# A causal convolution and a GELU layer on one core: five buffers for convolved blocks, all first taps on ScalarE, and half of one sum by transfer

## Chip, core and metric

The kernel runs on one core of a Trainium2 chip. The metric is device microseconds of one execution. The engines are named as in the profile: PE is the TensorE's matmuls (PEld its weight loads), DVE is VectorE, ACT is ScalarE, POOL is GpSimd, SP is SyncE, which here only issues transfers.

## What is computed

The input x has 8 sequences of 4096 tokens with 192 channels. Each of 8 heads (24 channels) has seven weights, which are normalized by a softmax; every channel is convolved with them over the last seven tokens. The result goes through a layer of 2048 hidden values with an exact GELU.

```python
w = np.exp(weight - np.max(weight, axis=-1, keepdims=True))
w = w / (np.sum(w, axis=-1, keepdims=True) + 1e-09)           # (8 heads, 7 taps)
x_pad = np.concatenate([np.zeros((B, 6, D)), x], axis=1)
idx = np.arange(S)[:, None] + np.arange(7)[None, :]
x_unf = x_pad[:, idx, :].reshape(B, S, 7, H, 24)
y = np.einsum('hk,bskhg->bshg', w, x_unf).reshape(B * S, 192)
h = y @ w_in                                                  # (32768, 2048)
g = 0.5 * h * (1.0 + erf(h / sqrt(2)))
out = g @ w_out                                               # (32768, 192), float32
```

## The kernel before, in words

**Blocks.** The 32768 tokens are cut into two halves that are worked on side by side, and each half into 35 blocks: blocks 0 to 5 with 256 tokens, blocks 6 to 34 with 512. Channels lie on partitions, the two halves together fill 128 partitions, and 192 channels make three planes of 64.

**Stages of a block n.** (1) SP loads x into one of three buffers `xin` (`load`). (2) DVE transposes it into `xT` (`trans`, written `tN` in the order), and POOL copies the six tokens before the block to its head (`halo`). (3) Seven taps make the convolution: the first tap multiplies into `acc`, six more multiply and add (`tap`, L345), and the last writes bf16 into `xc`. A first tap is made by DVE (L340), in two pieces, or by ACT (`first_tap`, L1123), one piece for each plane, written `f0`, `f1`, `f2`; which is set by `AT1` and `CALLS`. For blocks 0 and 1 PE makes the convolution. (4) The first product, `mm1` (L1258), multiplies `xc` with `win` in 16 slices into two PSUM buffers `hp` that alternate; after each slice ACT applies the GELU (L1165) and writes `gT`. (5) The second product of block n-1 is put piece by piece between the slices of block n. (6) Its result is transposed by DVE out of PSUM into `osb` (the `ev` steps), and SP stores it.

**Two kinds of second product.** From block 6 to 33, ten blocks make it directly (`mm2_t`, L1343, 48 rounds of four matmuls). The 18 blocks of the list `ST` make it with seven products instead of eight, in the manner of Strassen (`mm2_s`, L1392, 44 rounds). For those, sums of the GELU results are needed beforehand. They are cut into pieces of the eight column groups:

- `S1.0`, `S1.1`, `S1.2`: sum of two quarters of `gT`, by DVE (L699).
- `S3.0`, `S3.1`: one quarter of `gT` is added to another by an accumulating transfer that POOL issues (L671); `S3.2` is made by DVE (L702).
- `Dn.0`, `Dn.1`: a quarter plus `S1`. `Dn.1` is made by DVE (L705). `Dn.0` comes by transfer where the block before is a direct one (nine blocks): POOL copies the quarter (`cp`, L682) and then adds `S1` with an accumulating transfer (L686). In the other nine blocks DVE makes it (L705).
- `S4.0`, `S4.1`: a quarter plus `Dn`, by DVE (L708).

The products are named P1 to P7, D, E and e in `UNIT`; `TILES` gives the order in which each quarter of the PE works them off, in parts of which 5.5 make a block's second product. P6 reads Dn, P3 reads S4, P7 reads S3, P5, E and e read S1, and P4 needs the step k0. Afterwards the results are combined: ACT copies `p15`, `e`, `u`, `p3` out of PSUM (L743), POOL sends `u` across partitions twice (`cu` into `uu` and `cg` into `gsm` or `p5s`, L666), and DVE makes `k0` (L751), `k4` (L764, frees a PSUM bank, waits for `cg`) and `k3` (L758, waits for `cu`).

**What sets the order.** Each engine works its instructions off in the order of the program. For DVE it is written out by hand in `LIST`: row n holds the taps of block n (the bare digits), the transposes `tN`, and the steps of earlier blocks, `name.piece.block`. For ACT, `SLOT` says before which GELU of a block an extra instruction stands (`10:f1.13` before GELU 10). For POOL it is `GLIST`. SP loads some blocks ahead and then stores block n-1, in one loop; a load waits until DVE has transposed the block that had its buffer. A tap 6 waits until the first product of the last block with the same `xc` buffer is done:

```python
dst = ap(xc[n % 2], p0 * TB, [[NP * TB, 128], [TB, pn], [1, w]])
e.wait_ge(S_MM1, SL0[n - 1])
```

A copy `cp` waits, among others, until S4 of the seven-product block before is made, since all share one buffer `Dn`.

Of the kernel before, what the change touches and what calls it, by code (L numbers as in the profile page):

```python
# [11 lines left out]
def bass_lightweight_conv__then__act_gelu_exact_kernel(  # L12
# [91 lines left out]
    SLOT = {
        7: "2:f0.9 3:f1.9 5:f2.9",
        8: "3:f0.10 3:f1.10 6:f2.10 13:f0.11",
        9: "5:f1.11 6:p15.8 10:f2.11 13:f0.12 14:e.8",
        10: "0:f1.12 2:u.8 3:p3.8 4:f2.12 6:f0.13 10:f1.13",
        11: "1:f2.13 6:p15.10 13:e.10",
        12: "0:p3.10 2:u.10 6:p15.11 8:f2.14 11:f0.15 13:e.11 14:f1.15",  # L110
        13: "1:p3.11 2:u.11 4:f2.15 11:f0.16",
        14: "1:f1.16 4:f2.16 6:p15.13 9:f2.17 14:e.13",
        15: "0:p3.13 2:u.13 6:p15.14 13:e.14",
        16: "0:u.14 2:p3.14 4:f0.18 6:f1.18 8:f2.18 10:f0.19 13:f1.19",
        17: "7:p15.16 10:f2.19 12:f2.20 14:e.16",
        18: "0:p3.16 2:u.16 6:p15.17 13:e.17",
        19: "0:u.17 2:f0.21 4:p3.17 6:f1.21 8:f2.21",
        20: "5:f0.22 6:p15.19 10:f1.22 10:f2.22 13:e.19 14:f2.23",
        21: "0:p3.19 2:u.19 6:p15.20 13:e.20 15:f0.24",
        22: "2:u.20 4:p3.20 5:f1.24 8:f2.24 11:f0.25",  # L120
        23: "5:f1.25 6:p15.22 10:f2.25 13:e.22 14:f0.26",
        24: "0:u.22 2:p3.22 4:f1.26 4:f2.26 12:f0.27",
        25: "1:f1.27 4:f2.27 6:p15.24 14:e.24",
        26: "0:p3.24 2:u.24 6:p15.25 11:f2.28 13:f0.29 14:e.25",
        27: "0:p3.25 2:f1.29 4:u.25 6:f2.29",
        28: "0:f0.30 2:f1.30 6:p15.27 10:f2.30 13:f0.31 14:e.27",
        29: "0:f1.31 2:f2.31 3:u.27 4:p3.27 8:f0.32 10:f1.32 13:f2.32",
        30: "6:p15.29 14:e.29",
        31: "0:p3.29 2:u.29 4:f0.33 7:p15.30 8:f1.33 9:f2.33 13:e.30",
        32: "0:p3.30 2:u.30 4:f0.34 7:p15.31 9:f1.34 10:f2.34 15:e.31",  # L130
        33: "0:p3.31 2:u.31 6:p15.32 13:e.32",
# [58 lines left out]
    with es:  # L190
# [17 lines left out]
        xc = [sbt("xc%d" % i, [128, NP * TB], BF16) for i in range(2)]  # L208
# [450 lines left out]
        def st_dma(e, m, name, q):  # L659

            if name in ("cu", "cg"):
# [4 lines left out]
                e.dma_start(dst[UP, :], uu[LO, :]).then_inc(S_AD[name], 16)  # L666
                return
            if name == "S3":
# [842 lines left out]
```

## Time and profile before

| | |
|---|---|
| median of 3 runs | 666.59 us (666.11 to 667.13) |
| the profiled execution | 666.53 us, span of its instructions 664.8 us |
| busy: PE, DVE, ACT, POOL | 658.9, 623.6, 591.1, 105.5 us |
| granted TensorE clock | 1.00 |
| first GELU of blocks 31, 32, 33, 34 | 570.87, 591.87, 611.76, 631.65 us |
| GELU (L1165), mean of one | 1022 ns, 510 counted |
| tap on DVE (L345, 128x1536), mean of one in 84 to 632 us | 1806 ns |
| first tap on ACT (L1123, 128x512), mean of one | 714 ns |

The span runs from the first to the last instruction of the program; the rest of the execution's time lies around it. Busy time of PE is the union of matmuls that overlap in a pipeline, and so says little on how much faster PE could be. A row of the profile gives line, engine, operation, tiles and shapes, then the count, busy time, mean duration, and the idle time in front with what ended it.

### The profile page before, as it was taken

How to read it: one execution, taken by the hardware profiler on the slowest of the kernel's cores; microseconds unless marked ns; L12 is line 12 of the kernel's file. 1: busy time of each engine (PE TensorE's matmuls, PEld its weight loads, DVE VectorE, ACT ScalarE, POOL GpSimd, SP SyncE). 2: the span in 40 equal slices, each digit the busy share in tenths (PEclk: the TensorE clock that was granted, in tenths of full speed). 3: DMA queues.
4: the chain of work that ended last, by engine and by line, in shares of the span. 5: the costliest groups of instructions: out<-in, count | busy, mean ns of one | idle time of the engine just before them, and what ended most of it. 6: DMA issues, size and time to landing. Idle time of an engine off the chain costs nothing.

```text
span 664.8 us, 27970 instructions
## 1 busy us (share of the span) xinstructions
PE 658.9 (99%) x12792; PEld 478.9 (72%) x12792; DVE 623.6 (94%) x564; ACT 591.1 (89%) x691; POOL 105.5 (16%) x175
## 2 busy tenths in 40 slices
PE   9999999999999999999999999999999999999997
PEld 8999655576776677778777666757666757677776
DVE  5989999999999999999999999999999999999962
ACT  8899988898899898989889998989898998999882
POOL 8000540102010110202120102110102030111010
DMA  9746675645914691596189145959245838352454
GB/s 156 162 96 133 109 121 122 136 98 130 216 40 113 156 193 34 138 206 124 38 192 221 34 106 120 195 115 225 45 98 136 184 82 192 66 113 50 92 134 112
DMA packets 146438, 83.66 MB, mean 126 GB/s; under 512 B 129936, under 2 KB 138192, under 8 KB 146320
## 3 DMA queue, kind: packets, MB, share of 16 engines
q1 hardware_dynamic: 129328, 49.42, 33.7%
q0 software_dynamic: 15872, 31.86, 23.7%
q8 instruction: 100, 1.64, 1.0%
q10 hardware_dynamic: 1120, 0.59, 0.3%
q14 instruction: 18, 0.15, 0.1%
HBM read 31.51 MB, written 25.17 MB: 85 GB/s over the span
## 4 chain that ended last, share of the span: by engine, by line
PE 94%; DMA 2%; DVE 2%; POOL 1%; issue 1%; ACT 0%; DVEq 0%; POOLq 0%; ACTq 0%
PE hp L1258 48%; PE ob L1392 25%; PE ob L1343 16%; PE ob L1298 4%; DVE acc L345 1%; PE hp L1448 1%; DMA win<-in_moe_w_in_dram 1%; DMA xin<-in_x_dram 1%; PE ob L1448 1%; DMA uu<-uu 0%; ACT gT L1165 0%; POOL win L839 0%; DVE xT L984 0%; POOL xTb L360 0%; DVE xc L345 0%
## 5 line engine op out<-in xcount | busy, mean ns | idle before, releaser
L1165 ACT ACTIVATE gT<-hp 128x1024 bf16<-128x1024 f32 x510 | 514.6, 1022 | 60.1 <-PE hp L1258 52.7
L1258 PE MATMUL hp<-xc,win 64*64 64x512 bf16 (+2 forms) x6036 | 432.6, 366 | 0.5 <-DVE xc L345 0.4
L1258 PEld LDWEIGHTS hp<-xc,win 64*64 64x64 bf16 (+1 forms) x6036 | 229.1, 105 | 88.6 <-ACT gT L1165 5.9
L345 DVE SCALAR_TENSOR_TENSOR acc<-xT,wcol,acc 128x1536 f32<-128x1536 f32 (+1 forms) x165 | 282.3, 1711 | 7.4 <-ACT acc L1123 4.6
L1392 PE MATMUL ob<-gT,wot 64*64 64x512 bf16 x1152 | 219.6, 376 | 0.0
L1392 PE MATMUL ob<-gT,wst 64*64 64x512 bf16 (+2 forms) x1152 | 203.1, 323 | 0.7 <-DVE p5s L764 0.7
L1343 PE MATMUL ob<-gT,wot 64*64 64x512 bf16 x1920 | 133.5, 376 | 0.0
L1392 PE MATMUL ob<-s_S,wot 64*64 64x128 bf16 (+2 forms) x864 | 132.5, 305 | 0.0
L1392 PEld LDWEIGHTS ob<-gT,wst 64*64 64x64 bf16 x1152 | 98.5, 107 | 16.3 <-DVE p5s L764 1.6
L1392 PEld LDWEIGHTS ob<-gT,wot 64*64 64x64 bf16 x1152 | 89.5, 107 | 10.9 <-DVE osb L776 0.5
L1343 PEld LDWEIGHTS ob<-gT,wot 64*64 64x64 bf16 x1920 | 63.9, 107 | 39.7 <-DVE osb L776 0.3
L1392 PEld LDWEIGHTS ob<-s_S,wot 64*64 64x64 bf16 x864 | 68.6, 107 | 15.9
L1392 PE MATMUL ob<-s_Dn,wst 64*64 64x512 bf16 x288 | 79.5, 376 | 0.0
L1392 PE MATMUL ob<-s_S,wst 64*64 64x512 bf16 x288 | 79.5, 376 | 0.0
L671 POOL DMA_DIRECT2D gT<-gT x36 | 32.1, 902 | 198.3 <-DVE s_S L699 198.3
L984 DVE STREAM_TRANSPOSE xT<-xin 128x1536 f32<-128x1536 f32 (+2 forms) x39 | 59.4, 1532 | 3.5 <-DMA xin<-in_x_dram 2.8
L345 DVE SCALAR_TENSOR_TENSOR xc<-xT,wcol,acc 128x1536 bf16<-128x1536 f32 (+1 forms) x33 | 56.7, 1717 | 0.8
L1123 ACT ACTIVATE acc<-xT,wcol 128x512 f32<-128x512 f32 (+1 forms) x77 | 53.5, 698 | 0.0
L699 DVE TENSOR_TENSOR s_S<-gT 128x1024 bf16<-128x1024 bf16 (+1 forms) x54 | 45.8, 853 | 2.6 <-PE ob L1392 1.2
L708 DVE TENSOR_TENSOR s_S<-gT,s_Dn 128x2048 bf16<-128x2048 bf16 x36 | 43.1, 1218 | 0.4
L1298 PE MATMUL ob<-wout,gT 64*128 64x192 bf16 x768 | 42.0, 243 | 0.0
L892 POOL COPY xT<-xT 128x18 f32<-128x18 f32 x29 | 14.9, 514 | 156.8 <-DVE xc L345 145.1
(92 smaller groups left out, 416.1 us busy)
## 6 DMA issues: line engine op xcount, KB each, us to landing
out_dram<-osb SPq DMA_DIRECT2D x124, 192.0 KB, 3.5
xin<-in_x_dram SPq DMA_DIRECT2D x116, 192.0 KB, 4.2
gT<-gT POOLq DMA_DIRECT2D x18, 512.0 KB, 5.1
s_Dn<-gT POOLq DMA_DIRECT2D x9, 512.0 KB, 2.9
gT<-gT POOLq DMA_DIRECT2D x18, 256.0 KB, 4.1
s_Dn<-s_S POOLq DMA_DIRECT2D x9, 512.0 KB, 5.6
uu<-uu POOLq DMA_DIRECT2D x18, 128.0 KB, 2.6
xin<-in_x_dram SPq DMA_DIRECT2D x18, 96.0 KB, 2.5
```

Source lines behind the costliest of these rows:

```text
L345: return e.scalar_tensor_tensor(dst, src, wk, a, op0=ALU.mult, op1=ALU.add)
L671: e.dma_start(quad(m, 1, 0, k, k1 - k), quad(m, 0, 0, k, k1 - k), accum_op=ALU.add).then_inc(S_AD["S3.%d" % q], 16)
L699: ins = v.tensor_tensor(t("S1"), quad(m, 1, 0, k, n), quad(m, 1, 1, k, n), ALU.add)
L708: ins = v.tensor_tensor(t("S4"), quad(m, 0, 1, k, n), t("Dn"), ALU.add)
L892: g.tensor_copy(dst, src).then_inc(S_HALO)
L984: v.transpose(out, src).then_inc(S_TR)
L1123: a.activation(out=acc[n % 2][:, p * TB : p * TB + w], in_=ap(xT[n % 2], p * XW + HX, [[NP * XW, 128], [1, w]]), func=AF.Copy, scale=wcol[ ...
L1165: a.activation(out=ap(gT[n % 2], (i % 2 * NF + i // 2) * TB if n in ST else i * c * 2 * w, dst), in_=ap(ob, 2 * TB, [[4 * TB, 128], *src[1 ...
L1258: ins = t.matmul(hbuf(u, slice(fo, fo + fw), o, w), ap(win, f1, [[NP * F, 64], [2, fw]]), xc[n % 2][r, p * TB : p * TB + w], start=(p == 0 ...
L1298: ins = t.matmul(bb[sub], gT[m % 2][r, c0 : c0 + 128], wout[r, CH[sub][i] * C : (CH[sub][i] + 1) * C], start=(ph == 0 and k == 0), stop=(p ...
L1343: ins = t.matmul(bank(BK[m][j], slice(64 * h, 64 * h + 64), w), ap(wot, 64 * hf * NF * C + CH[h][i] * C + 64 * j, [[NF * C, 64], [1, 64]]) ...
L1392: ins = t.matmul(bank(BK[m][bk], slice(64 * cg, 64 * cg + 64))[:, c0 : c0 + w], wt_, x, start=(e == mine[0]), stop=(e == mine[-1] or e in ...
```

## The change

- `xc` has five buffers instead of two; tap 6 of block n waits for the first product of block n-5.
- ACT makes all three first tap pieces of every block from 4 on (93 instead of 77). DVE made both pieces for blocks 7 and 8 and one piece for 14, 17, 20, 23 and 28.
- `Dn.0` comes by transfer in all 18 seven-product blocks. Every second one uses a buffer of its own, `dn2`; `u` is also kept in two buffers in turn, `uu` and `u2`, each with its own semaphores.
- `LIST` now begins at row 4 and holds the preparation of the weights (`w`) and the evictions of block 5, which stood in a list of their own; `LIST`, `SLOT` and `GLIST` are written anew. SP's lead is given for each block in `AHEAD`.

`c1` and the transfer of `S1` in the new code are issued by no entry of the lists. The core of the diff, with the rows that the prediction speaks of:

```diff
+    NXC = 5
+    AHEAD = {4: 10, 6: 13, 7: 14, 8: 14, 9: 16, 10: 18, 11: 18, 12: 20, 13: 20, 14: 20, 15: 22, 16: 22, 17: 23, 18: 25, 19: 25, 21: 27, 22: 28, 23: 30, 24: 30, 26: 33, 27: 35, 28: 35, 29: 35}
...
+        4: "w.0.0 t5 1 w.1.0 2 3 4 5 6",
+        5: "t6 1 2 3 4 5 6",
+        6: "1 t7 2 3 w.2.0 w.3.0 4 5 w.4.0 6",
+        7: "1 2 3 4 5 t8 w.5.0 w.6.0 6",
+        8: "t9 evac.0.5 evac.1.5 w.7.0 1 2 3 4 w.8.0 w.9.0 ev.0.6 5 6",
...
-        32: "ev.0.27 Dn.1.29 S4.0.29 S3.2.29 ev.2.28 1 S4.1.29 2 k0.0.29 S1.0.30 3 t33 4 ev.2.29 Dn.0.30 S1.1.30 S1.2.30 5 6",
-        33: "S3.2.30 k3.0.29 k4.0.29 Dn.1.30 S4.0.30 S4.1.30 ev.1.29 ev.0.29 k0.0.30 1 S1.0.31 2 ev.2.30 S1.1.31 3 S1.2.31 t34 S3.2.31 Dn.0.31 4 k4.0.30 Dn.1.31 S4.0.31 S4.1.31 k3.0.30 k0.0.31 5 6",
-        34: "S1.0.32 S1.1.32 1 ev.2.31 ev.0.30 S1.2.32 Dn.0.32 S4.0.32 Dn.1.32 ev.1.30 S3.2.32 k4.0.31 S4.1.32 2 3 k0.0.32 4 5 S1.0.33 k3.0.31 6",
+        32: "ev.1.28 S1.2.29 Dn.1.29 ev.2.28 k3.0.27 ev.1.27 S3.2.29 1 S4.0.29 S4.1.29 2 k0.0.29 3 S1.0.30 4 5 S1.1.30 ev.2.29 t33 S1.2.30 Dn.1.30 S3.2.30 6",
+        33: "k4.0.29 S4.0.30 k3.0.29 ev.0.29 S4.1.30 ev.1.29 k0.0.30 t34 1 S1.0.31 S1.1.31 2 ev.2.30 3 S1.2.31 4 5 S3.2.31 k4.0.30 Dn.1.31 S4.0.31 S4.1.31 k0.0.31 k3.0.30 ev.0.30 ev.1.30 6",
+        34: "S1.0.32 S1.1.32 1 ev.2.31 2 S1.2.32 S3.2.32 3 Dn.1.32 k4.0.31 4 ev.0.31 S4.0.32 S4.1.32 k0.0.32 k3.0.31 ev.1.31 5 S1.0.33 6",
...
+        7: "1:f0.8 2:f1.8 3:f2.8 8:f0.9 9:f1.9 11:f2.9",
+        12: "0:p3.10 2:u.10 4:f0.14 6:p15.11 8:f1.14 9:f2.14 13:e.11 14:f0.15",
+        31: "0:p3.29 2:u.29 4:f0.33 6:p15.30 8:f1.33 10:f2.33 12:f0.34 13:e.30",
...
-        xc = [sbt("xc%d" % i, [128, NP * TB], BF16) for i in range(2)]
+        xc = [sbt("xc%d" % i, [128, NP * TB], BF16) for i in range(NXC)]
+        dn2 = sbt("dn2", [128, NF // 4 * TB], BF16)
+        u2 = sbt("u2", [128, TB], F32)
...
-                dst = ap(xc[n % 2], p0 * TB, [[NP * TB, 128], [TB, pn], [1, w]])
-                e.wait_ge(S_MM1, SL0[n - 1])
+                dst = ap(xc[n % NXC], p0 * TB, [[NP * TB, 128], [TB, pn], [1, w]])
+                if n >= NXC:
+                    e.wait_ge(S_MM1, SL0[n - NXC + 1])
...
-        BYDMA = {'N': 'S3.0 S3.1 Dn.0', 'S': 'S3.0 S3.1'}
+        BYDMA = {'N': 'S3.0 S3.1 Dn.0', 'S': 'S3.0 S3.1 Dn.0'}
...
-                if ST.index(m):
-                    e.wait_ge(*summed(ST[ST.index(m) - 1], "S4", k))
+                j = ST.index(m) - 2 + min(q, 1)
+                if j >= 0:
+                    e.wait_ge(*summed(ST[j], "S4", k))
...
-            "cu.0.25 cp.0.27 cg.0.25 S3.0.27 Dn.0.27 S3.1.27 halo.31 halo.32 cg.0.27 "
-            "cu.0.27 cp.0.29 S3.0.29 S3.1.29 Dn.0.29 halo.33 S3.0.30 S3.1.30 cu.0.29 "
-            "cg.0.29 S3.0.31 S3.1.31 cg.0.30 cu.0.30 halo.34 S3.0.32 S3.1.32 cg.0.31 "
-            "cu.0.31 S3.0.33 S3.1.33 cg.0.32 cu.0.32 cg.0.33 cu.0.33 "
+            "cu.0.27 S3.0.29 cp.0.29 Dn.0.29 S3.1.29 halo.32 halo.33 cp.0.30 S3.0.30 "
+            "Dn.0.30 S3.1.30 cg.0.29 cu.0.29 halo.34 cp.0.31 S3.0.31 S3.1.31 Dn.0.31 "
+            "cg.0.30 cu.0.30 cp.0.32 S3.0.32 S3.1.32 cg.0.31 Dn.0.32 cu.0.31 cp.0.33 "
+            "S3.0.33 S3.1.33 cg.0.32 Dn.0.33 cu.0.32 cg.0.33 cu.0.33 "
...
-                while xs < min(NB, n + 5 + (1 if n >= 8 else 0)):
+                while xs < min(NB, AHEAD.get(n, n + 5)):
```

More of the change, by code (lines that the diff above doesn't have):

```diff
@@ L75, in bass_lightweight_conv__then__act_gelu_exact_kernel @@
     LIST = {
[27 rows of a table removed]
[32 rows of a table added]
     }
     SLOT = {
[L105 to L112, printed above, removed]
-        15: "0:p3.13 2:u.13 6:p15.14 13:e.14",
@@ L114, in bass_lightweight_conv__then__act_gelu_exact_kernel @@
[L114 to L131, printed above, removed]
+        2: "3:f0.4 5:f1.4 6:f2.4",
@@ new lines, in bass_lightweight_conv__then__act_gelu_exact_kernel @@
+        3: "1:f0.5 3:f1.5 4:f2.5 7:f0.6",
+        4: "1:f1.6 3:f2.6",
+        5: "1:f0.7 3:f1.7 6:f2.7",
+        7: "1:f0.8 2:f1.8 3:f2.8 8:f0.9 9:f1.9 11:f2.9",
+        8: "2:f0.10 3:f1.10 7:f2.10",
+        9: "1:f0.11 6:p15.8 9:f1.11 10:f2.11 12:f0.12 13:e.8 15:f1.12",
+        10: "1:p3.8 3:f2.12 3:u.8 6:f0.13 8:f1.13 9:f2.13",
+        11: "7:p15.10 13:e.10",
+        12: "0:p3.10 2:u.10 4:f0.14 6:p15.11 8:f1.14 9:f2.14 13:e.11 14:f0.15",
+        13: "0:p3.11 3:u.11 4:f1.15 5:f2.15 7:f0.16 11:f1.16",
@@ new lines, in bass_lightweight_conv__then__act_gelu_exact_kernel @@
+        14: "0:f2.16 7:p15.13 10:f0.17 10:f1.17 13:e.13 14:f2.17",
+        15: "0:p3.13 2:u.13 6:p15.14 13:e.14",
+        16: "0:f0.18 2:p3.14 3:u.14 5:f1.18 6:f2.18 9:f0.19 11:f1.19",
+        17: "3:f2.19 6:p15.16 10:f0.20 10:f1.20 13:e.16 14:f2.20",
+        18: "0:p3.16 2:u.16 6:p15.17 14:e.17 15:f0.21",
+        19: "0:u.17 2:p3.17 3:f1.21 5:f2.21 8:f0.22 9:f1.22 11:f2.22",
+        20: "6:p15.19 10:f0.23 11:f1.23 13:e.19 14:f2.23",
+        21: "0:p3.19 2:u.19 6:p15.20 13:e.20",
+        22: "1:p3.20 4:u.20 4:f0.24 6:f1.24 9:f2.24 10:f0.25",
@@ new lines, in bass_lightweight_conv__then__act_gelu_exact_kernel @@
+        23: "3:f1.25 6:p15.22 9:f2.25 12:f0.26 13:e.22 15:f1.26",
+        24: "1:f2.26 3:u.22 4:p3.22 7:f0.27 11:f1.27",
+        25: "1:f2.27 6:p15.24 13:e.24 14:f0.28",
+        26: "0:p3.24 2:u.24 6:p15.25 8:f1.28 9:f2.28 13:e.25 14:f0.29",
+        27: "1:p3.25 4:u.25 4:f1.29 6:f2.29 9:f0.30",
+        28: "4:f1.30 7:p15.27 8:f2.30 9:f0.31 14:e.27 15:f1.31",
+        29: "1:u.27 2:f2.31 4:p3.27 8:f0.32 12:f1.32",
+        30: "3:f2.32 6:p15.29 14:e.29",
+        31: "0:p3.29 2:u.29 4:f0.33 6:p15.30 8:f1.33 10:f2.33 12:f0.34 13:e.30",
@@ L132, in bass_lightweight_conv__then__act_gelu_exact_kernel @@
+        32: "0:p3.30 2:u.30 6:p15.31 10:f1.34 10:f2.34 15:e.31",
+        33: "0:p3.31 2:u.31 7:p15.32 13:e.32",
         34: "0:p3.32 2:u.32 7:p15.33 15:e.33 15:u.33",
@@ L135, in bass_lightweight_conv__then__act_gelu_exact_kernel @@
     SLOT = {n: [(int(i), k, int(m)) for i, k, m in (q.replace(":", ".").split(".") for q in s.split())] for n, s in SLOT.items()}
-    AT1 = {4: (3, 5, 6), 5: (3, 5, 6), 6: (2, 3, 5)}
-    for n in range(M0 + 3, NB):
+    AT1 = {}
+    for n in range(4, NB):
         AT1[n] = [(b, i) for b in SLOT for i, k, m in SLOT[b] if k[0] == "f" and m == n]
@@ L263, in bass_lightweight_conv__then__act_gelu_exact_kernel @@
         S_DP = sem("S_DP")
-        S_AD = {k: sem("S_AD" + k) for k in ("S3.0", "S3.1", "S3.2", "Dn.0", "Dn.1", "cp.0", "cp.1", "cu", "cg")}
+        S_AD = {k: sem("S_AD" + k) for k in ("S3.0", "S3.1", "S3.2", "S1.0", "c1.0", "Dn.0", "Dn.1", "cp.0", "cp.1", "Dn.0b", "cp.0b", "cu", "cg", "cub", "cgb")}
         block = es.enter_context(nc.Block())
@@ L306, in conv_out @@
             o = p * TB + c0 + d0
-            dst = xc[n % 2][ro, o : o + dw]
+            dst = xc[n % NXC][ro, o : o + dw]
             cb = 512 * cbank(n, kd) + d0
@@ L562, in bass_lightweight_conv__then__act_gelu_exact_kernel @@
                     key, one = (p, 16) if p in BYDMA[m] else (name, 1)
+                    if p == "Dn.0" and one > 1:
+                        key += "b" * (ST.index(m) % 2)
                     count[key] = count.get(key, 0) + one
@@ L568, in summed @@
             return SUM_AT[m, name, [k < q for q in SUMS[name][1:]].index(True)]
-        SIDE = [((M0 + 2, 4 * g // 2, 0), "evac", M0 - 1, g) for g in range(NG[M0 - 1])]
-        SIDE += [((M0 - 1, 2 * k + 1, 0) if k < NP else (M0 + 1 + (k - NP) // 4, 2 + (k - NP) % 4, 0), "w", 0, k) for k in range(10)]
-        SIDE.sort(key=lambda q: q[0])
+        SIDE = []
         for b in LIST:
@@ L647, in quad, with sums @@
             return ap(gT[m % 2], ((2 * par + h) * (NF // 2) + k) * TB, [[NF * 2 * TB, 128], [1, n * TB]])
+        def sums(m, name, k, n, r=slice(0, 128), c0=0):
+            if name == "Dn" and k < NF // 4 and ST.index(m) % 2:
+                return dn2[r, k * TB + c0 :][:, :n]
+            return sst[name][r, k * TB + c0 :][:, :n]
         def st_read(e, m, name, q):
-            if m - 1 in ST and (name, q) in FORM[m - 1][5]:
+            if m - 1 in ST and (name, q) in FORM[m - 1][5] and (name, q) != ("Dn", 0):
                 EVENTS, _, DONE, _, _, READ = FORM[m - 1]
@@ L664, in st_dma @@
                     e.wait_ge(S_DP, dp(m, "k0"))
-                dst = uu if name == "cu" else gs(m)
-                e.dma_start(dst[UP, :], uu[LO, :]).then_inc(S_AD[name], 16)
+                dst = us(m) if name == "cu" else gs(m)
+                e.dma_start(dst[UP, :], us(m)[LO, :]).then_inc(S_AD[name + "b" * (ST.index(m) % 2)], 16)
                 return
@@ L674, in st_dma @@
                 return
+            if name in ("c1", "S1"):
+                k, k1 = SUMS["S1"][q : q + 2]
+                d = ap(sst["S1"], k * TB, [[NF // 2 * TB, 128], [1, (k1 - k) * TB]])
+                if name == "c1":
+                    e.wait_ge(S_GELU, SL0[m] + 2 * k1)
+                    st_read(e, m, "S1", q)
+                    if ST.index(m):
+                        e.wait_ge(*summed(ST[ST.index(m) - 1], "Dn", k))
+                    e.dma_start(d, quad(m, 1, 0, k, k1 - k)).then_inc(S_AD["c1.%d" % q], 16)
+                else:
+                    e.wait_ge(S_AD["c1.%d" % q], SUM_AT[m, "S1", q][1])
+                    e.dma_start(d, quad(m, 1, 1, k, k1 - k), accum_op=ALU.add).then_inc(S_AD["S1.%d" % q], 16)
+                return
             k, k1 = SUMS["Dn"][q : q + 2]
-            d, s1 = (ap(sst[x], k * TB, [[NF // 2 * TB, 128], [1, (k1 - k) * TB]]) for x in ("Dn", "S1"))
+            odd = "b" * (q == 0 and ST.index(m) % 2)
+            d, s1 = (sums(m, x, k, (k1 - k) * TB) for x in ("Dn", "S1"))
             if name == "cp":
@@ L693, in t @@
             def t(x):
-                return ap(sst[x], k * TB, [[NF // 2 * TB, 128], [1, n * TB]])
+                return sums(m, x, k, n * TB)
             v.wait_ge(S_GELU, SL0[m] + 2 * k1)
@@ L713, in gs, with us @@
             return (gsm, p5s)[ST.index(m) % 2]
+        def us(m):
+            return (uu, u2)[ST.index(m) % 2]
         def tqs(m):
@@ L731, in st_copy @@
                     "p15": (gs(m)[:, :], bank(BK[m]["X"])),
-                    "u": (uu[LO, :], xb(LO)),
+                    "u": (us(m)[LO, :], xb(LO)),
                     "p3": (tqs(m)[LO, :], xb(UP)),
@@ L739, in st_copy @@
                 a.wait_ge(S_EV, EV[ST[i - 2], 1])
-            if name == "u" and i:
-                a.wait_ge(S_DP, dp(ST[i - 1], "k3"))
-                a.wait_ge(S_AD["cg"], 16 * i)
+            if name == "u" and i > 1:
+                a.wait_ge(S_DP, dp(ST[i - 2], "k3"))
+                a.wait_ge(S_AD["cg" + "b" * (i % 2)], 16 * (i // 2))
             a.activation(out=dst, in_=src, func=AF.Copy, scale=-1.0 if name == "p15" else 1.0).then_inc(S_AC)
@@ L752, in st_post @@
             elif name == "k3":
-                v.wait_ge(S_AD["cu"], 16 * ST.index(m) + 16)
+                v.wait_ge(S_AD["cu" + "b" * (ST.index(m) % 2)], 16 * (ST.index(m) // 2) + 16)
                 v.wait_ge(S_AC, ac(m, "p3"))
@@ L758, in st_post @@
                 ins = v.scalar_tensor_tensor(
-                    tqs(m)[:, :], uu[:, :], sgn[:, 0:1], tqs(m)[:, :], op0=ALU.mult, op1=ALU.add
+                    tqs(m)[:, :], us(m)[:, :], sgn[:, 0:1], tqs(m)[:, :], op0=ALU.mult, op1=ALU.add
                 )
@@ L762, in st_post @@
                 v.wait_ge(S_MM2, MMC[m + 1])
-                v.wait_ge(S_AD["cg"], 16 * ST.index(m) + 16)
+                v.wait_ge(S_AD["cg" + "b" * (ST.index(m) % 2)], 16 * (ST.index(m) // 2) + 16)
                 ins = v.tensor_tensor(gs(m)[:, :], bank(BK[m]["Y"]), gs(m)[:, :], ALU.subtract)
@@ L1008, in _ @@
             for n in range(2, NB):
-                if n < M0 + 3:
+                if n < 4:
                     ops = [] if n in K0 else [("t", n, 0)]
@@ L1063, in extra @@
                     st_add(v, n, name, q)
-            side = [q for q in SIDE if q[0][0] < M0 + 3]
+            side = [q for q in SIDE if q[0][0] < 4]
             for b in range(2, NB):
@@ L1112, in _ @@
             first = {}
-            for n, at in AT1.items():
-                if n < M0 + 1:
-                    for j, q in enumerate(at):
-                        first[n - 2, q] = (n, j)
             def first_tap(n, p):
@@ L1260, in mm1 @@
                                 ap(win, f1, [[NP * F, 64], [2, fw]]),
-                                xc[n % 2][r, p * TB : p * TB + w],
+                                xc[n % NXC][r, p * TB : p * TB + w],
                                 start=(p == 0 and (cc == 0 or not head)),
@@ L1382, in mm2_s @@
                     need(*summed(m, src, k))
-                    x = sst[src][r, k * TB + c0 :][:, :w]
+                    x = sums(m, src, k, w, r, c0)
                 g = CG[0][k]
```

6 lines of the change are left out of this document (3 added, 3 removed), and 68 rows, old and new, of tables (GLIST, LIST).

## The prediction

> **What bounds the kernel now.** I read the page's first part, then the chain of waits in order of time for the pace of TensorE (PE), then busy time by stretches of one block, then the timeline where one stretch is longer than its like.
>
> ```profile
> PE 658.9 (99%) x12792; PEld 478.9 (72%) x12792; DVE 623.6 (94%) x564; ACT 591.1 (89%) x691; POOL 105.5 (16%) x175
> ...
> 110.36 0.86 PE ob L1343 x16
> 111.22 0.65 PE hp L1258 x12
> ```
>
> Matmuls overlap, so 99% busy alone proves nothing. The pace does: 16 matmuls of 512 columns in 0.86 us, 12 in 0.65, hence 54 ns each while one lasts 376 ns: four quarters of the array work at once, 0.215 us for each four, at granted clock 1.00. What can be won is therefore only time in which PE stands still. To find it I compare block periods (first GELU of a block to the next one's first GELU). Each of the two stretches below holds 192 first-product matmuls and one seven-product sum:
>
> ```profile
> 570.87:591.87 21.00, 20.28 (x406) 14.38 (x401) 19.46 (x20) 18.98 (x23) 3.76 (x5) 1.00 0.41 90
> 591.87:611.76 19.89, 19.89 (x406) 15.59 (x399) 19.76 (x19) 18.96 (x24) 3.11 (x5) 1.00 0.26 52
> ```
>
> Columns: length, then busy time and count of PE, PEld, DVE, ACT, POOL. The same 406 matmuls take 1.11 us more in block 31. Summing such differences over blocks 7 to 33 (like against like, from the times between the ends of first-product groups) I find 0.93 + 0.25 in block 31, 0.12 in block 12, 0.09 in block 17, and nothing else over 0.08 us. The stall itself:
>
> ```profile
> 573.57 0.56 POOL L666 DMA_DIRECT2D uu<-uu  x1 [1.29 <-ACT uu L743]
> 574.16 0.56 POOL L666 DMA_DIRECT2D p5s<-uu  x1
> ...
> 576.87 0.75 DVE L758 SCALAR_TENSOR_TENSOR wtf<-uu,sgn,wtf 128x512 f32<-128x512 f32 x1 [1.08 <-DMA uu<-uu]
> 577.54 0.68 DVE L764 TENSOR_TENSOR p5s<-ob,p5s 128x512 f32<-128x512 f32 x1
> ...
> 578.28 0.35 PE L1392 MATMUL ob<-gT,wst 64*64 64x128 bf16 x2 [0.72 <-DVE p5s L764]
> ```
>
> POOL issues cu.0.29 before cg.0.29; VectorE (DVE) runs k3.0.29 (L758), which waits 1.08 us for cu, before k4.0.29 (L764), and PE waits 0.72 us for the bank that k4 frees. So PE is the bound, with some 1.4 us of stalls in 550; DVE, 94% busy, has hardly any slack (its last convolved block ends at 630.17, 0.3 us before PE wants it), which is why single delays reach PE.
>
> **The sum** starts at the profiled execution: 666.53 us, its span of 664.8 and 1.7 around it. The median of the three runs is 666.59, so no correction.
>
> **First taps to ScalarE (ACT).** Removed from DVE (L340): seven of 128x1024 and two of 128x512, 7 x 0.71 + 2 x 0.47 = 5.9 us. Added to ACT: 16 of 128x512.
>
> ```profile
> L1123 ACT ACTIVATE acc<-xT,wcol 128x512 f32<-128x512 f32 x68 | 48.3, 714 | 0.0
> L705 DVE TENSOR_TENSOR s_Dn<-gT,s_S 128x2048 bf16<-128x2048 bf16 x25 | 30.2, 1211 | 0.1
> ```
>
> 16 x 0.71 = 11.4 us on ACT. Cover: it sits idle 52.7 us in front of GELUs waiting for PE. The fullest new block (12, as 31) has 16 GELUs, 4 first taps and p3, u, p15, e. Two GELUs take 1.94 us in the timeline, one 1.02, so the pitch is 0.92; with the same 0.1 off the others: 14.7 + 2.4 + 1.6 = 18.7, under the 19.9 of a block. Block 7 gets six taps, 18.4 of 20.7. Three of them stand ahead of successive GELUs; ACT then falls behind by 3 x (0.92 + 0.61 - 1.29) = 0.7 us, and the two hp buffers allow some 0.9 (two turns of 1.29 less a first product of 0.65 and a GELU of 1.02). On the path: 0. Without that cover each further tap would cost PE 0.6.
>
> **Half of Dn by transfer in nine more blocks.** DVE sheds 9 x 1.21 = 10.9 us (L705). POOL gets nine cp (0.55 to issue) and nine Dn (1.03), 14.2 us, of which its 16% load makes nothing. What counts is order. Behind a Dn waiting for its cp to land stand S3, cg and cu; and transfers issued on top of each other are slow:
>
> ```profile
> gT<-gT POOLq DMA_DIRECT2D x18, 512.0 KB, 5.1
> s_Dn<-gT POOLq DMA_DIRECT2D x9, 512.0 KB, 2.9
> s_Dn<-s_S POOLq DMA_DIRECT2D x9, 512.0 KB, 5.6
> ...
> DMA to landing us min/median/max: 4.5/5.6/7.9
> ```
>
> The last line is Dn's (L686): 7 to 8 when issued within 1 us of an S3, 4.5 to 5.3 mostly otherwise. In most blocks P6, the reader of Dn, starts some 12 us into the next block, and 7 us or more are left: 0. The chain that is short is Dn, S4, P3 in the run of seven-product blocks 29 to 33, where the new list puts Dn.0.32 behind cg.0.31. That moment stands in the trace:
>
> ```profile
> 613.58 0.58 ACT L743 ACTIVATE uu<-ob 64x512 f32<-64x512 f32 x1
> 614.52 0.56 POOL L666 DMA_DIRECT2D p5s<-uu  x1 [4.60 <-ACT uu L743]
> 615.12 0.55 POOL L666 DMA_DIRECT2D uu<-uu  x1
> ```
>
> p5s<-uu is cg.0.31; Dn.0.32 takes the place of the next line, 615.1. Landing 4.5 to 5.3 later: 619.6 to 620.4. S4.0.32 (L708, 1.22): 620.8 to 621.6. Need: P3 starts at 2.75 of the 5.5 parts of block 33's PE time, which begins at about 611.1 (first GELU 611.76 less 0.65): 621.0. DVE reaches S4.0.32 at about 620.0 (ev.2.31 at 611.0, then four taps of 1.8 and five small operations). So 0 to 0.6 us of stall here and, by the same order (cg.0.32 ahead of Dn.0.33), 0 to 0.5 in block 34. With Dn at 7.9 it would be 3.2 and some 3. Nothing excludes a gain, but PE has nothing to gain here beyond the stalls counted below. I take 0.2 for both together, since no S3 is issued within 4 us of either Dn.
> [...]
>
> **New order on DVE and POOL at block 31.** The new lists put cg.0.29 ahead of cu.0.29 and k4.0.29 ahead of k3.0.29. cg then issues at 573.57, lands 2.2 (its median) to 3.0 later (as here), 575.8 to 576.6; k4 ends by 576.4 to 577.3; PE ran dry between 577.1 and 577.6. Gain 0.9 to 1.1; I take 1.1. S1.1.30, whose S3 is queued ahead of cg, now has 6.5 us of DVE work between it and k4, more than the 4.5 of that issue and landing. Blocks 12 and 17: 0.1 of 0.2.
>
> **Five xc buffers.** Tap 6 of block n waits for first products of n-5, not n-2. In the trace DVE never waits there (before xc it is idle 0.8 us in 33). The list still does block n beside the sums of n-2, so the lead doesn't grow: 0. **Second buffers** u2, dn2: u and cp wait one seven-product block less; POOL's early waits aren't on the path: 0. **Loads ahead (SP).** A store now stands behind later loads. Worst: store of block 26 behind load 34, which waits for t31; that is 5.4 us of DVE work after ev.1.26, and its buffer is wanted two lists later: 0. **Weights and block 6's evictions earlier.** DVE waits 3.0 us at 45.3 for a first tap of block 5, which now comes earlier; that pays for the three w of list 4 to 6 (0.34 to 0.61 each). xc of block 6 ends near 65.6 instead of 66.2. In list 8, ev.0.6 waits for PE's second pass over block 6, with taps 5 and 6 behind it: xc of block 8 near 101.4, wanted at 104.5: 0.
>
> Sum: 666.53 - 1.1 - 0.1 + 0.2 = 665.5.
>
> **Rivals.**
> (1) DVE is the bound and its 16.8 us come off: 649.7. For: 94% busy, no slack. Against: PE's pace is the same in every block, and block 32 shows DVE busy 19.76 of 19.89 with PE never still. Chance 0.02. [...]
> (2) The stall at block 31 stays or moves, since a transfer from POOL lands late elsewhere (uu<-uu took 7.8 in one place): 666.5. Chance 0.14. Equally if the change doesn't do what it says and leaves DVE's turn as it was.
> (3) Slower: Dn queued against S3. Where Dn.0 stands straight ahead of S3.0 (blocks 11, 24, 27), S3.0 lands in up to 8.0 instead of 5.1, and Dn in 7.9. From a landing of 5.0 on, each us costs one in block 33 and one in block 34; S3.0.24 (issue near 443.9, wanted near 451.0) adds up to 0.9. All at the maximum: 666.53 - 1.2 + 3.2 + 3.0 + 0.9 = 672.4; with half of it 668.9. It decides from a mean landing of 6.3, where it costs 2.5 and the forecast's gain of 1.2 is outweighed by 1.3. Chance 0.20.
>
> **Numbers.** Forecast 0.64, spread 664.8 to 666.0. A measurement here tells about 0.2%, 1.33 us, from no change; so faster means under 665.2. Of the forecast's chance 0.30 lies below that, 0.34 above; rival 1 adds 0.02 to faster, rival 2 0.14 to same, rival 3 0.04 to same and 0.16 to slower. Faster 0.32, same 0.52, slower 0.16. The range runs from the forecast's lower end, 664.8, to 667.9, so leaving out rival 1 and most of rival 3.
>
> **What would show it.** Right: block 31 takes 19.9 us, no PE wait on k4; DVE falls to near 607 us busy with waits of its own, ACT rises to about 602; PE's pace unchanged. Wrong: a PE wait for s_S or s_Dn in blocks 33 and 34, S3 landings over 6 in blocks 11, 24, 27, or ACT late in block 7.

## The result: 0.7% slower, and where PE stands still now

The changed kernel takes 671.38 us (median of 6 runs, 670.32 to 672.82), the kernel before 666.78 beside it: ratio 1.0072, interval 1.0059 to 1.0085. The profiled execution took 671.19 us with a span of 669.5, 4.7 more than before. 665.5 was forecast, with a range to 667.9.

The engines' instruction counts changed as planned: 18 fewer on DVE, 16 more on ACT, 18 more on POOL. The first line of the page:

```profile
PE 660.9 (99%) x12792; PEld 486.7 (73%) x12792; DVE 611.1 (91%) x546; ACT 598.8 (89%) x707; POOL 122.8 (18%) x193
```

DVE is 12.5 us less busy (16.8 were forecast), ACT 7.7 (11.4) and POOL 17.3 (14.2) more, and the kernel is slower all the same. PE's pace is unchanged: block 7 takes 20.72 us in both. From the first GELU of block 7 to that of block 34 the changed kernel takes 551.8 us, 547.1 before; these 4.7 us are the whole loss. Against the shortest like time between the ends of first-product groups, block 12 loses 2.2 us, 32 1.1, 21 0.9, 31 0.8; 20, 25, 30 and 33 lose 0.4 to 0.5 each. Together PE loses some 8 us in blocks 7 to 33, some 3 before (where the prediction listed the larger ones, 1.4). Block 12 from first GELU to first GELU, before and after:

```profile
187.04:206.43 19.39, 19.39 (x394) 13.65 (x390) 19.13 (x18) 18.31 (x23) 1.43 (x5) 1.00 0.16 33
186.64:208.59 21.95, 20.45 (x405) 14.18 (x399) 19.17 (x18) 19.52 (x24) 2.19 (x3) 1.00 0.76 170
```

Before, PE was busy throughout; now it is busy for 20.45 of 21.95 us. The last two numbers say that the DMA engines were 16% busy and moved 33 GB/s in this block, and now are 76% busy and move 170. Block 31, the place of the old stall, in the timeline:

```profile
576.80 0.56 POOL L686 DMA_DIRECT2D p5s<-u  x1 [2.82 <-ACT u L782]
...
580.57 0.69 DVE L803 TENSOR_TENSOR p5s<-ob,p5s 128x512 f32<-128x512 f32 x1 [1.96 <-DMA p5s<-u]
...
581.32 0.35 PE L1428 MATMUL ob<-gT,wst 64*64 64x128 bf16 x2 [0.51 <-DVE p5s L803]
```

cg.0.29 is now issued first, as planned, but it lands at 580.47, 3.7 us after its issue; DVE sits idle for 1.96 us in front of k4 (now L803), and PE waits for k4. The block takes 20.6 us, 21.0 before, where 19.9 was forecast. The same pattern stands in blocks 12, 21 and 32. All the instructions of line k4, the kernel before first:

```profile
  DMA p5s<-uu: 3.5, 3
who waited for it (us, times):
  PEld ob L1392: 1.6, 2
  PE ob L1392: 0.7, 1
```

and after the change:

```profile
  DMA p5s<-u: 9.5, 4
  DMA gsm<-uu: 5.8, 6
who waited for it (us, times):
  PEld ob L1428: 5.0, 4
  PE ob L1428: 3.0, 4
```

The first rows tell DVE's idle time in front of k4 until cg had landed: 3.5 us in 3 places before, 15.3 in 10 after. From issue to landing, all cu and cg, minimum, median and maximum before:

```profile
DMA to landing us min/median/max: 2.2/2.5/7.8
```

and after:

```profile
DMA to landing us min/median/max: 2.2/3.5/6.1
```

The worst place is block 12, where a load and a store of SP come on top:

```profile
188.44 1.90 SPq L825 DMA_DIRECT2D xin<-in_x_dram  x4
189.35 0.56 POOL L686 DMA_DIRECT2D p5s<-u  x1 [6.39 <-ACT u L782]
190.39 4.57 SPq L845 DMA_DIRECT2D out_dram<-osb  x4
...
195.21 0.35 PE L1428 MATMUL ob<-gT,wst 64*64 64x128 bf16 x2 [1.40 <-DVE p5s L803]
```

Load 17 waits until 188.44 for its buffer, and the store of block 9 stands behind it, as the prediction saw for other blocks and priced at nothing. cg.0.10 (issued 189.35) lands after 5.0 us instead of the 2.2 of before, and PE stands still for 1.4 us.

### The profile page after: what moved, and what is told of

The parts are those of the page before. It is cut to its first block, busy times and chain, and to the rows that moved or that the text cites. A ratio compares the mean times of both kernels' runs of the same rounds, so it can differ in the third digit from the quotient of the medians.

```text
span 669.5 us, 27992 instructions
## 1 busy us (share of the span) xinstructions
PE 660.9 (99%) x12792; PEld 486.7 (73%) x12792; DVE 611.1 (91%) x546; ACT 598.8 (89%) x707; POOL 122.8 (18%) x193
## 4 chain that ended last, share of the span: by engine, by line
PE 86%; issue 5%; DMA 4%; POOL 2%; ACT 1%; DVE 1%; DVEq 0%; POOLq 0%; ACTq 0%
PE hp L1294 44%; PE ob L1428 21%; PE ob L1379 15%; PE ob L1334 5%; DMA p5s<-u 2%; PE ob L1484 1%; PE hp L1484 1%; DMA win<-in_moe_w_in_dram 1%; POOL gT L691 1%; ACT gT L1201 1%; DMA gsm<-uu 1%; DMA s_Dn<-gT 1%; DVE p5s L803 0%; POOL s_Dn L721 0%; POOL win L880 0%
## 5 line engine op out<-in xcount | busy, mean ns | idle before, releaser
L1294 PE MATMUL hp<-xc,win 64*64 64x512 bf16 (+2 forms) x6036 | 440.3, 366 | 0.1
L1294 PEld LDWEIGHTS hp<-xc,win 64*64 64x64 bf16 (+1 forms) x6036 | 236.1, 105 | 83.1 <-ACT gT L1201 5.0
L1428 PEld LDWEIGHTS ob<-gT,wot 64*64 64x64 bf16 x1152 | 89.6, 107 | 8.4 <-DVE osb L815 1.0
L1379 PEld LDWEIGHTS ob<-gT,wot 64*64 64x64 bf16 x1920 | 66.1, 107 | 37.5
L1159 ACT ACTIVATE acc<-xT,wcol 128x512 f32<-128x512 f32 (+1 forms) x93 | 65.0, 702 | 0.0
L1428 PE MATMUL ob<-s_Dn,wst 64*64 64x512 bf16 x216 | 61.0, 376 | 0.0
L1334 PEld LDWEIGHTS ob<-wout,gT 64*128 64x128 bf16 x768 | 35.0, 94 | 3.3
L933 POOL COPY xT<-xT 128x18 f32<-128x18 f32 x29 | 19.8, 689 | 88.3 <-DVE xc L359 77.8
```

What stands on the lines that cost most here:

```text
L933: g.tensor_copy(dst, src).then_inc(S_HALO)
L1159: a.activation(out=acc[n % 2][:, p * TB : p * TB + w], in_=ap(xT[n % 2], p * XW + HX, [[NP * XW, 128], [1, w]]), func=AF.Copy, scale=wcol[ ...
L1294: ins = t.matmul(hbuf(u, slice(fo, fo + fw), o, w), ap(win, f1, [[NP * F, 64], [2, fw]]), xc[n % NXC][r, p * TB : p * TB + w], start=(p == ...
L1334: ins = t.matmul(bb[sub], gT[m % 2][r, c0 : c0 + 128], wout[r, CH[sub][i] * C : (CH[sub][i] + 1) * C], start=(ph == 0 and k == 0), stop=(p ...
L1379: ins = t.matmul(bank(BK[m][j], slice(64 * h, 64 * h + 64), w), ap(wot, 64 * hf * NF * C + CH[h][i] * C + 64 * j, [[NF * C, 64], [1, 64]]) ...
L1428: ins = t.matmul(bank(BK[m][bk], slice(64 * cg, 64 * cg + 64))[:, c0 : c0 + w], wt_, x, start=(e == mine[0]), stop=(e == mine[-1] or e in ...
```

## The experiments

Theory A: the transfers crowd the DMA engines, cg lands late, k4 with it. A1 puts the crowd down to SP's lead, A2 to the nine added Dn. Theory B: the loss lies in the new order on DVE. Each time is a median; ratios are to the kernel before on the same chip.

**The nine Dn, and SP's lead, undone.** In e1_lead SP has its old lead:

```diff
-                while xs < min(NB, AHEAD.get(n, n + 5)):
+                while xs < min(NB, n + 5 + (1 if n >= 8 else 0)):
```

> The changed kernel, but SP loads with the lead of before. Two theories of where the 4.7 us went. Theory A, two kinds of crowding: PE waits for k4, and k4 for the transfer cg, which lands late, (A1) in block 12 because a load and a held-back store burst onto the DMA engines just then, (A2) in blocks 20, 21, 25 and 30 to 33 because Dn and S3 stand ahead of cg in POOL's own queue. Theory B: the new order of DVE's list itself is late, whatever the transfers do. A1 alone expects here 1.5 to 2.2 us less than the changed kernel, 669.2 to 669.9, cg.0.10 landing in under 3.5 us instead of 5.0, and the other stalls as they were. B expects no change, 671.4.

In e2_dn the nine new Dn.0 go back to DVE, each right ahead of Dn.1 or S4.0 of its block, and their cp and Dn leave POOL's list (block 30 as an example):

```diff
-        32: "... S1.2.30 Dn.1.30 S3.2.30 6",
+        32: "... S1.2.30 Dn.0.30 Dn.1.30 S3.2.30 6",
-            "... cp.0.30 S3.0.30 Dn.0.30 S3.1.30 ..."
+            "... S3.0.30 S3.1.30 ..."
```

> The changed kernel, but the nine new halves of Dn are made by DVE again, as before, and their cp and Dn transfers are gone; lead, five buffers, first taps on ScalarE and the rest of the order stay. A2 expects the stalls of blocks 20, 21, 25 and 30 to 33 to go, some 3 to 4 us of 671.4, hence 667.5 to 668.5, with block 12 still short of 2 us; DVE about 11 us busier. B expects 671 or more, since DVE gets more to do.

e3_lead_dn has both edits.

> Both undone at once: old lead, nine halves of Dn on DVE. If A1 and A2 are the whole cost, 665.5 to 666.5, level with the kernel before; what is above that belongs to the order, the buffers or the first taps. B expects 671.

Measured: e1_lead 681.26 us, 1.0223 (1.0192 to 1.0253); e2_dn 671.06, 1.0062 (1.0050 to 1.0074); e3_lead_dn 674.06, 1.0104 (1.0089 to 1.0120). e1 and e3 are slower than either theory expected; e2 misses A2 and lands where B put it. The old lead isn't harmless but far worse here; PE's waits in e1_lead:

```profile
PE ob L1428 <- DMA gT<-gT: 8.2, 4, 3.2
```

With the loads at other moments S3 lands later (its 512 KB in a median of 5.8 us instead of 4.9), and PE waits for it up to 3.2 us at a time. So the lead given for each block belongs to the change: it keeps S3 from landing late, while a load and a store fall on cg.0.10. In e2_dn the landing of cu and cg is back at a median of 2.6 us, and k4 costs PE less (its weight loads wait 3.4 us instead of 5.0):

```profile
  PE ob L1428: 0.6, 2
```

but the time stays: 551.4 us from block 7 to block 34, where the changed kernel takes 551.8. What PE gains there it loses elsewhere: it waits for S4 (L743) in blocks 18, 21 and 33, for S3 in block 30 and for an eviction in block 23, while DVE has 9 us more to do (620.1 busy). A2 is neither shown nor refuted by this run; undoing a part of a new order is not the part alone.

**The Dn transfers without their bytes.** e12_dn_small keeps every instruction and wait, but the nine new accumulating transfers move 32 of 2048 columns (the rest of that half of Dn then lacks S1):

```diff
+                if m in (11, 14, 17, 20, 25, 30, 31, 32, 33):
+                    d, s1 = d[:, :32], s1[:, :32]
                 e.dma_start(d, s1, accum_op=ALU.add).then_inc(S_AD["Dn.%d" % q + odd], 16)
```

> The changed kernel, but in the nine blocks that newly take Dn.0 by transfer the accumulating transfer moves only the first 32 of 2048 columns (the rest of that half of Dn lacks S1); order, waits and all other transfers stay. Theory A (the Dn transfers crowd cg): the k4 stalls of blocks 21, 31 and 32 shrink from 0.5, 0.7 and 0.9 to under 0.3, block 12's stays near 2 (no Dn is under way there), 669.3 to 670.3. Theory B (cg is late for another reason, S3.1 or the loads): 671 to 671.8, landings of cg.0.19, cg.0.29 and cg.0.30 unchanged at 3.7 to 4.0.

Measured: 667.18 us, 1.0004 (0.9994 to 1.0014). The bytes of nine transfers cost 4.2 us (4.5 by the ratios), nearly the whole loss, more than A expected. Landing of cu and cg, and PE's wait for k4 (3.0 us in 4 places in the changed kernel):

```profile
DMA to landing us min/median/max: 2.2/2.6/6.4
...
  PE ob L1430: 1.0, 2
```

Block 12 gains most (2.2 to 1.0 us of loss): in the changed kernel a Dn was under way after all, Dn.0.11, issued at 180.3, on top of which S3.0.11 and S3.1.11 took 8.0 us each; here they take 5.5 and 5.3, and cg.0.10 lands after 3.7 us instead of 5.0. Blocks 21 and 32 gain 0.7 each; block 31 hardly anything (0.8 to 0.7), the expectation there missed. These four blocks, the ones with a wait for k4, gain 2.8 us together. The rest of the 4.2 can't be read from this profile: its execution took 668.61 us, 1.4 more than the median. The run also says something on DVE's work: e2_dn, which makes the same nine halves on DVE, takes 3.9 us more than this one. In this order the halves thus cost nearly the same as transfers (4.2) and on DVE (3.9), which is why e2_dn showed no difference.

**Dn by transfer alone.** e7_before_dn has lists, slots, lead and two xc buffers as before the change, and only the nine Dn by transfer, with `u2` and `dn2` (block 32 as an example):

```diff
-        34: "... S1.2.32 Dn.0.32 S4.0.32 Dn.1.32 ..."
+        34: "... S1.2.32 S4.0.32 Dn.1.32 ..."
-            "... S3.0.32 S3.1.32 ..."
+            "... cp.0.32 S3.0.32 S3.1.32 Dn.0.32 ..."
```

> Lists, ACT slots, SP lead and two xc buffers as before the change; only Dn.0 of the nine other seven-product blocks comes by transfer (cp ahead of S3.0, Dn behind S3.1 on POOL, dn2 and u2 in use). Theory A (the added transfers crowd the DMA engines, so that cg and S3, which PE needs within some 3 to 5 us, land late): 668.5 to 671, with PE standing behind k4 L803 in the blocks that follow a pair of seven-product blocks (12, 15, 18, 21, 31 to 33), cg landing 3.5 to 5 instead of 2.2 to 3.0. Theory B (the loss sits in the new order of DVE and SP, the transfers themselves are harmless): 666.0 to 667.0.

Measured: 688.63 us, 1.0335 (1.0310 to 1.0361), far over what A expected. Timeline of block 33:

```profile
617.78 1.50 POOL L714 DMA_DIRECT2D s_Dn<-s_S  x1
...
625.73 1.23 DVE L736 TENSOR_TENSOR s_S<-gT,s_Dn 128x2048 bf16<-128x2048 bf16 x1 [5.16 <-ACT gT L1197]
...
629.34 0.63 PE L1424 MATMUL ob<-gT,wst 64*64 64x512 bf16 x1 [3.22 <-DVE gT L730]
```

Dn.0.32 lands 7.8 us after 617.78, at 625.60; DVE stands 5.2 us in front of S4.0.32 (the view puts that down to a GELU long done), S3.2.32 stands behind it, and PE waits 3.2 us for S3.2; 4.0 in the next block. In six other places PE waits for k4, 7.3 us together. The changed kernel, with the same nine transfers in its own order (lists, slots, lead and first taps together), is 17 of these 22 us faster. How much of the 22 lies in the place that the edit gave Dn, behind S3.1 on POOL and with DVE's rows left as they were, no run separates.

**An earlier cg, with no byte moved.** e9_u_first lets u and p3 change places in nine blocks; in e14_u0_p31 p3 follows in slot 1; e15_before_u0_p31 is the latter in the kernel before:

```diff
-        31: "0:p3.29 2:u.29 4:f0.33 ..."
+        31: "0:u.29 2:p3.29 4:f0.33 ..."      (e9)
+        31: "0:u.29 1:p3.29 4:f0.33 ..."      (e14, e15)
```

> The changed kernel, but where ACT copies p3 in slot 0 and u in slot 2 of a block the two change places (nine blocks), so cg is issued some 1.8 us earlier in blocks 12, 15, 18, 21, 26, 31, 32, 33, 34; no work and no transfer is added or removed. Theory A (the loss is k4 waiting for a late cg): the k4 stalls of blocks 12, 21, 31 and 32 shrink by up to 1.8 us each, together 2.2 to 3.2: 668.2 to 669.2. Theory B (the loss is DVE's own lateness in the new order): 671.0 to 671.8.

> The changed kernel with u copied in slot 0 and p3 in slot 1 (before: p3 in slot 0, u in slot 2). With u in slot 0 and p3 in slot 2 the k4 stalls were gone, but PE waited 0.6 us for p3 in each of nine blocks; in slot 1 p3 ends about 1 us earlier than there, ahead of PE's need by some 0.4. Theory A (the whole loss is k4 waiting for cg): the k4 stalls stay away and nothing replaces them, PE's excess in blocks 7 to 33 falls from 7.8 to 1.5-2.5 us, 665.0 to 666.6. Theory B (ACT, with two copies in a row ahead of GELU 1, becomes late, or another transfer is then the last): 669 to 671.

> The same exchange (u in slot 0, p3 in slot 1) in the kernel before. Theory A: k4's cg comes 1.8 us earlier there too, but only the 1.2 us of the stall at block 31 can be won: 665.2 to 666.6. Theory B: ACT late, 667.5 to 669.

Measured: e9_u_first 670.93 us, 1.0063 (1.0047 to 1.0079); e14_u0_p31 668.79, 1.0026 (1.0015 to 1.0037); e15_before_u0_p31 668.51, 1.0019 (1.0009 to 1.0029). None of the three lands where A put it; e15 lands where B did. In e9 k4 holds up PE nowhere any more, but p3 does, in nine places (waits for line L782, ACT's copies):

```profile
  PE ob L1428: 2.4, 9
```

e14 has neither wait (0.3 us of k4 in front of a weight load are left). It is 2.6 us faster than the changed kernel, less than A expected, since two copies in a row make ACT late: PE's weight loads wait 8.0 us for GELUs instead of 5.0. In e15 they wait 8.4 instead of 5.9, and the kernel before loses 1.6 us by it. If ACT's lateness costs the changed kernel the same, k4's lateness costs 2.6 + 1.6 = 4.2 us more there than before, as much as the bytes of the nine Dn. So theory A stands by two ways, the second with that condition.

**Another queue.** e4_cg_act issues cg from ACT's queue, right behind u:

```diff
                     st_copy(a, m, k)
+                    if k == "u":
+                        st_dma(a, m, "cg", 0)
```

> The changed kernel, but the transfer cg is issued from ScalarE's queue right behind the copy u, all else as it is. If cg is late because it stands behind Dn and S3 in POOL's queue, it lands in 2.2 to 2.7 us in blocks 21, 31 and 32 and their stalls of 2.2 us go: about 669.0. If it is late because the DMA engines are full whichever queue it comes from, its landing stays at 3.7 to 4.0 and the time at 671.4. The issue costs ScalarE some 0.4 us for each of 18 blocks, which its idle time covers. Block 12, with the engines full of loads, should stay slow by either.

Measured: 677.89 us, 1.0160 (1.0146 to 1.0173). DMA issues of that run:

```profile
gsm<-uu ACTq DMA_DIRECT2D x9, 128.0 KB, 4.0
...
p5s<-u ACTq DMA_DIRECT2D x9, 128.0 KB, 3.5
```

Medians of 3.5 and 4.0 us, no better than from POOL (3.0 and 3.3 in the changed kernel): cg isn't late because of its place in POOL's queue. The time is over both expectations, since ACT's idle time doesn't cover the issues: each holds ACT for 0.47 us, and PE's weight loads now wait 19.1 us for GELUs.

**Smaller parts.** e11_lead17 issues load 17 a block later, e6_xc2 has two xc buffers:

```diff
-    AHEAD = {... 10: 18, ...}
+    AHEAD = {... 10: 17, ...}      (e11)
-    NXC = 5
+    NXC = 2                        (e6)
```

> The changed kernel, but SP issues load 17 one block later (AHEAD of block 10 is 17, not 18), so that it no longer falls on S3.1.11 and cg.0.10, and the store of block 9 isn't held back behind it. Theory A1 (the burst of load 17 and the held store makes cg.0.10 late): block 12's excess of 2.2 us falls under 0.6 and nothing else moves, 669.6 to 670.2. Theory B (the burst is chance, some other crowding takes its place): 671.0 to 671.8.

> The changed kernel with two xc buffers instead of five. Both theories: 671.4, since DVE does block n beside the sums of n-2 in either order. If the five buffers matter at all, DVE waits in front of xc (L359, tap 6) for first products and the time is above 672.7.

Measured: e11_lead17 670.57 us, 1.0052 (1.0040 to 1.0064), block 12 loses 1.8 instead of 2.2 and cg.0.10 still lands after 4.7 us, a miss for A1; e6_xc2 670.77, 1.0054 (1.0042 to 1.0066). Neither can be told from the changed kernel (the intervals overlap). No worth of the xc buffers shows; load 17 has a small share of block 12 at most.

**The forecast's other terms, in the kernel before.** e17_before_cg29 has only the reordering at block 29, e19_before_taps only the first taps of five blocks on ACT, e20_before_taps_cg29 both:

```diff
-        33: "S3.2.30 k3.0.29 k4.0.29 ..."
+        33: "S3.2.30 k4.0.29 k3.0.29 ..."
-            "... S3.1.30 cu.0.29 cg.0.29 ..."
+            "... S3.1.30 cg.0.29 cu.0.29 ..."
-        14: "k4.0.10 0 S4.0.11 ..."
+        14: "k4.0.10 S4.0.11 ..."
-        12: "... 8:f2.14 11:f0.15 ..."
+        12: "... 8:f0.14 9:f1.14 10:f2.14 11:f0.15 ..."
```

> The kernel before with one reordering alone: cg.0.29 ahead of cu.0.29 on POOL, k4.0.29 ahead of k3.0.29 on DVE (the term of -1.1 of the forecast, without the added transfers). If that term was sized rightly: block 31 falls from 21.0 to about 19.9 us and the time by 0.9 to 1.2, 665.5 to 666.1. If the stall is set by something else there (S3.1.30 still landing, DVE late for k4 anyway): 666.6 to 667.1, block 31 still near 21.0.

> The kernel before with the first taps of blocks 14, 17, 20, 23 and 28 all on ACT (ten pieces of 128x512 more there, five pieces of 128x1024 fewer on DVE, 3.6 us); nothing else. If ACT's idle time hides them and DVE's relief has no stall of PE to remove: 666.3 to 667.1. If ACT becomes late in one of these blocks (its idle time in a block is 1 to 2 us): PE waits for gT and the time is over 667.5. If DVE's relief matters: under 666.

> The kernel before with both edits: the reordering for block 29 and the ten first taps on ACT. If each behaves as sized: 665.4 to 666.2, the fastest of the kernels here. If the taps cost as much as the reordering brings: 666.6 to 667.5.

Measured: e17 666.92 us, 1.0000 (0.9991 to 1.0009); e19 669.96, 1.0045 (1.0032 to 1.0057); e20 669.15, 1.0039 (1.0027 to 1.0052), over both of its ranges. The reordering gains nothing by itself. In e17's profiled execution, which took 668.28 us, 1.4 over the median, block 31 even takes 21.9 us, and PE waits 0.94 us for k4, 0.72 before. The POOL transfers between 570 and 580 us, from issue to landing, before:

```profile
uu<-uu POOLq DMA_DIRECT2D x1, 128.0 KB, 3.3
p5s<-uu POOLq DMA_DIRECT2D x1, 128.0 KB, 3.0
```

and in e17, where cg goes first:

```profile
p5s<-uu POOLq DMA_DIRECT2D x1, 128.0 KB, 4.1
uu<-uu POOLq DMA_DIRECT2D x1, 128.0 KB, 3.9
```

In both, S3.1.30 was issued some 2.1 us earlier and is still under way. The two land within 0.4 us of each other in either order; the first in line wins nothing. In e19 PE's weight loads wait for GELUs:

```profile
PEld hp L1258 <- ACT gT L1165: 10.4, 37, 0.7
```

5.9 us before, 5.0 in the changed kernel with all its taps on ACT. My slots in rows 20 and 21 put taps next to p3, and block 21 alone loses 1.2 us more; a tap also stands ahead of u there, so cg is issued later, and a weight load waits 0.6 us for k4.

No run beat the kernel before.

## Why the prediction was wrong, step by step

- **PE is the bound, only its standstills count, DVE's relief is worth nothing by itself**: right against the kernel before. e12_dn_small has all of the relief (DVE 611.2 us busy, 623.6 before) without the bytes of the nine Dn, and takes the time of the kernel before (1.0004). Rival 1 is out.
- **Nine more Dn: "0" but for 0.2 in blocks 33 and 34.** This is the step that failed. Measured 4.2 us (e12_dn_small). I looked at who reads Dn (P6, S4) and at what stands behind it on POOL, and there the step nearly held. Dn.0.32 and Dn.0.33 land 4.7 us after their issue, within the 4.5 to 5.3 taken, and P3's weight load comes 0.46 us late in each of blocks 33 and 34, where 0.2 was forecast for both. In block 34 S4.0.33 had waited for Dn; the load that reads it starts 0.12 us after S4.0.33 ends:

```profile
644.05 1.22 DVE L743 TENSOR_TENSOR s_S<-gT,dn 128x2048 bf16<-128x2048 bf16 x1 [2.40 <-DMA dn<-s_S]
...
645.39 0.14 PEld L1428 LDWEIGHTS ob<-s_S,wot 64*64 64x64 bf16 x2 [0.46 <-issue]
```

  What I didn't ask is whom the bytes slow down that are under way at the same time. It is above all cg, a transfer of a quarter of the size: in the four blocks that stall, ACT copies u in slot 2, cg is issued right behind it, and some 3.5 us are left from there until k4 has to start for PE. Also misread was when a Dn is slow: of the seven issued within 1 us of an S3 before, four took 7.0 to 7.9 us, the other three 4.5 to 5.3.
- **cg.0.29 lands in 2.2 to 3.0: gain 1.1 at block 31.** The term was mis-sized: 3.7 us in the changed kernel, 4.1 in e17, whose gain is 0; the changed kernel's block 31 is 0.4 us shorter than before. The 2.2 is cg's median over all blocks; behind S3.1 and beside cu it doesn't hold.
- **SP's lead: "0".** Not shown to be right: a store behind a load fell on cg.0.10. Its share of block 12's 2.2 us isn't separated from that of Dn.0.11; e11 took 0.4 away, e12 1.2. And the old lead would have cost 10 us (e1_lead): the 0 was true only of the reader that I looked at, the buffers.
- **First taps: 0**: right for the change's own slots as far as the traces tell (weight loads wait 5.0 us for GELUs, 5.9 before; no run has these taps alone), and e19 shows that the cover of 52.7 us is no pool to draw on: ten taps elsewhere cost 3.1 us, 0.3 each, half of the 0.6 that I named for taps without cover.
- **Five xc, second buffers: 0**: right for xc (e6_xc2). The second buffers weren't tried alone.
- **The rivals.** Rival 2 (the stall moves since a transfer lands late elsewhere) had the mechanism, with a price of 1.0 over the forecast where 5.9 was measured. Rival 3 had the price (672.4 at the maximum) and the bytes of Dn as the cause, but S3 and S4 as the places; in e7_before_dn, in the old order, S4 and S3.2 do stall so, beside k4.

The terms close: 665.5 forecast, 1.1 of gain that didn't come (e17), 4.2 for the Dn bytes (e12) make 670.8 of 671.4. The rest of 0.6 is within the noise of these terms. Open is what makes cg late in block 31, which the bytes of Dn hardly change.

## What to carry to other kernels

A transfer that takes work off an engine can take time from the transfers under way with it (the bytes of nine cost 4.2 us here): list the short transfers with a deadline (here cg, some 3.5 us ahead of the need) and ask which of them the new bytes fall on, not only who reads the new result. Don't price a landing by its median; take it from the moment in question, with all that is under way there. Where an engine's idle time is to hide added work, look for the slot: two extra instructions in a row cost PE time that the sum of idle time doesn't show (1.6 us in e15_before_u0_p31).

## What the runs showed of the hardware that was unexpected

In e7_before_dn PE ran at half pace after its two longest standstills. The 3 us after standstills of 1.97, 3.22 and 4.02 us:

```profile
379.60:382.60 3.00, 3.00 (x71) 2.36 (x75) 3.00 (x3) 1.20 (x2) 0.00 (x0) 1.00 0.02 5
629.30:632.30 3.00, 2.96 (x38) 2.01 (x42) 3.00 (x3) 1.18 (x2) 0.00 (x0) 0.50 0.82 198
656.50:659.50 3.00, 2.97 (x42) 1.91 (x46) 3.00 (x6) 0.58 (x1) 0.00 (x0) 0.55 0.26 63
```

The granted clock (third number from the right) is 0.50 and 0.55 after the longer ones, where half as many matmuls start (38 and 42, not 71), and 1.00 after the shortest. In e1_lead it was 0.60 over 134 to 137 us, where PE had been busy for only 1.13 of the 4 us before. Block 33 of e7_before_dn, which holds the standstill of 3.22 us and the stretch at 0.50, took 26.6 us from first GELU to first GELU, 19.9 before; none of the rivals' prices held that.
